# Keys of an attention in chunks of 128, the second head mixing on column halves, the products with the values by even and odd row tiles

## The chip, the cores and the metric

The kernel runs as one program on one core of a Trainium2 chip. The metric is the device time of one execution in microseconds. The times here are a median of several runs; the profile is one further execution of the same program, and its own time stands beside them below.

## What is computed

Attention with talking heads for 4 batches of 12 heads, 448 tokens and 64 columns, and behind it a gated network on all 1792 tokens. All inputs are float32.

```python
scores = scale * np.matmul(q, k.transpose(0, 1, 3, 2))
scores = np.einsum('bhij,hg->bgij', scores, w_pre)
scores = scores - np.max(scores, axis=-1, keepdims=True)
attn = np.exp(scores)
attn = attn / (np.sum(attn, axis=-1, keepdims=True) + 1e-09)
attn = np.einsum('bhij,hg->bgij', attn, w_post)
x = np.matmul(attn, v)            # then (tokens, 12 * 64)
out = (silu(x @ w_gate) * (x @ w_val)) @ w_out
```

## The kernel before

**Stages.** The attention fills about the first 480 us of the span, the gated network the rest. This change is in the attention alone.

**Attention.** For a batch `b`, `qk` (L216) makes the scores of 128 query rows for a pair of heads, `qkcopy` takes them out of PSUM and `store` writes them to a buffer in DRAM. `gather` reads them back so that one row group holds 5 tokens by 12 heads. The work then goes by tiles of 10 query rows (`TS`), two tiles `t` at a time, which is one unit `u`; there are 45 tiles and 23 units a batch, and the last unit has one tile. For each unit: `pre` (L270, first mixing, both tiles at once on quarters of the array), `top` (VectorE, the negated maximum), `expo` (ScalarE, the exponential `e` and its sum), `norm` (VectorE the reciprocal, GpSimd the scaled mixing weights `rw`), `post` (L306, second mixing) and `mixed` (ScalarE, from PSUM into `attnT`).

**Second mixing.** The keys lie in 4 chunks of 112 (`CP`), so that chunk `c` holds the keys p * 4 + c. `post` takes, for each tile and chunk, 112 columns of `e` as the stationary operand and the 120 columns of `rw` as the moving one.

**Values.** `attnT` is a ring of 3 segments of 112 tokens. `av` (L328) multiplies it with the values `vn`, for two segments (224 tokens) and one pair of heads at a time: 4 chunks by 2 heads, the heads on the two column halves of the array, into one buffer of the tag `tr`. The last batch does its last two segments singly. `values` (batches 0, 2, 3) and `second_values` (batch 1) copy the result out of PSUM, on ScalarE and VectorE. The tag `tr` has two buffers in PSUM; `kprep` (L174, name `ktr`) and `qprep` (L191, `qtr`), which transpose the keys and the queries of the next batch, use it too.

**Order.** `at(key, fn)` records every step with a key, and the program is written out in the order of the keys; each engine then runs its own instructions in that order, and waits for semaphores. A unit `u` of a batch has the key n = 45 b + 2 u, which the following calls a slot. In a slot: `pre` at n + 0.5, `qk` of the next rows at n + 0.65, `post` of the unit before at n + 1.2, the transposes at n + 1.25, `av` at n + 1.3, `values` from n + 1.9. The products of the first two segments begin in slot 13 of their batch, with two pairs of heads in that slot and one in each of the next four; those of the last two run in slots 1 to 5 of the next batch.

**Loads.** All loads and stores are issued by SyncE (SP), in order. `load_v` (L144) brings the values of 3 heads, and runs four times from n0 + 16.9 on (n0 = 45 b), one call every 1.95. `load_k` (L162) brings the next batch's keys for a pair of heads, two slots ahead of `kprep`; its tile `kn` has two buffers, so the load for pair p waits until `kprep` has read pair p - 2. In the listings of the order below, `[waits DMAHW3_49]` is a wait for a DMA: there are eight such semaphores, taken in turn, and a DMA on SP that takes one waits until the DMA eight places before it has landed.

## Time and profile before

| | |
|---|---|
| median of 3 runs | 999.2 us (998.84 to 1002.1) |
| the profiled execution | 991.94 us, its span 990.2 us |
| PE (TensorE) busy | 951.3 us, 96% of the span |
| VectorE, ScalarE, GpSimd busy | 642.2, 429.1, 248.1 us |
| granted TensorE clock, mean | 0.996 |
| second mixing on PE (L306) | 1440 records, 170.8 us |
| products with the values on PE (L328) | 864 records, 81.6 us |
| DMA rs<-s_d in the chain that ended last | 3% of the span |

The busy time of PE is no measure of how close PE is to its limit, since records overlap: what a group of matmuls costs is read from where it starts to where the next group starts. Each float32 matmul stands in the trace as two records. PEld is the loading of stationary operands. SPq rows are DMA issues; their length is the time of issuing alone.

### The profile page before, as it was taken

What the parts mean: (1) busy time and instruction counts of PE and PEld (TensorE: products, weight loads), DVE (VectorE), ACT (ScalarE), POOL (GpSimd) and SP (SyncE); (2) the same over time, 40 slices, a digit from 0 to 9 for tenths busy, and PEclk for the clock granted to TensorE, in tenths of its full rate; (3) what the DMA queues carried; (4) which work ended last, traced back from release to release, by engine and by line L of the source; (5) the groups of instructions that cost most, each with busy time, mean ns of one, the idle gap of its engine ahead of it and who ended that gap; (6) DMA issues with size and microseconds to landing.
All of it is one profiled execution on the core that took longest, in us unless ns stands there. A gap on an engine that the chain in (4) does not pass through costs nothing.

```text
span 990.2 us, 18171 instructions
## 1 busy us (share of the span) xinstructions
PE 951.3 (96%) x6732; PEld 757.2 (76%) x6732; DVE 642.2 (65%) x1130; ACT 429.1 (43%) x961; POOL 248.1 (25%) x308
## 2 busy tenths in 40 slices
PE   4699999999999999999999999999999999999998
PEld 2356666656656666667899999999998999999998
DVE  2466555545555564567599999999927999984110
ACT  1366566646565564656334334332223444442110
POOL 2011111133331111122244434443313333320000
PEclk9899999999999999999999999999999999999999
DMA  6799888999799676884255454459663112122311
GB/s 174 212 280 263 260 246 254 269 239 318 223 326 251 204 219 181 244 226 131 80 171 164 144 179 156 144 187 339 235 238 98 61 65 65 65 65 65 118 38 38
DMA packets 146292, 179.03 MB, mean 181 GB/s; under 512 B 51640, under 2 KB 121628, under 8 KB 146204
## 3 DMA queue, kind: packets, MB, share of 16 engines
q1 hardware_dynamic: 145948, 177.77, 59.4%
q8 instruction: 54, 0.88, 0.4%
q14 instruction: 34, 0.28, 0.1%
q0 software_dynamic: 256, 0.09, 0.0%
HBM read 108.59 MB, written 69.24 MB: 180 GB/s over the span
## 4 chain that ended last, share of the span: by engine, by line
PE 84%; DMA 7%; DVE 3%; ACT 2%; SPq 2%; POOL 1%; issue 1%; ACTq 0%; POOLq 0%; DVEq 0%
PE post L306 13%; PE pre L270 7%; PE qk L216 7%; PE dn L731 6%; PE dn L733 6%; PE dn L732 6%; PE av L328 6%; PE p L641 5%; PE p L644 5%; PE p L642 5%; DMA rs<-s_d 3%; PE upv L701 3%; PE upv L696 3%; PE upv L697 3%; PE upg L701 3%; PE upg L696 3%
## 5 line engine op out<-in xcount | busy, mean ns | idle before, releaser
L306 PEld LDWEIGHTS post<-rw,e 128*112 128x112 f32 x1440 | 153.7, 177 | 65.9 <-issue 42.7
L306 PE MATMUL post<-rw,e 128*112 128x120 f32 (+1 forms) x1440 | 170.8, 272 | 6.1 <-POOL rw L298 3.8
L287 ACT ACTIVATE e<-pre,st 128x448 f32<-128x448 f32 x180 | 112.4, 629 | 109.8 <-DVE st L281 109.2
L298 POOL TENSOR_SCALAR rw<-w_post_gs,st 128x120 f32<-128x120 f32 x180 | 67.8, 388 | 338.3 <-DVE st L295 185.3
L281 DVE TENSOR_REDUCE st<-pre 128x1 f32<-128x448 f32 x180 | 104.1, 618 | 63.1 <-PE pre L270 62.4
L731 PE MATMUL dn<-whi,gh 128*128 128x256 f32 x504 | 141.1, 280 | 1.4 <-DVE u L648 1.4
L732 PE MATMUL dn<-wlo,gh 128*128 128x256 f32 x504 | 141.0, 280 | 0.0
L733 PE MATMUL dn<-whi,gl 128*128 128x256 f32 x504 | 141.0, 280 | 0.0
L552 POOL TENSOR_SCALAR mag<-mag 128x768 f32<-128x768 f32 x33 | 99.5, 3015 | 140.9 <-ACT mag L550 137.5
L270 PE MATMUL pre<-rs,w_pre_blocks 60*64 60x448 f32 x720 | 101.3, 565 | 11.1 <-DMA rs<-s_d 8.4
L315 ACT ACTIVATE attnT<-post 112x480 f32<-112x480 f32 (+3 forms) x192 | 97.0, 550 | 13.3 <-PE post L306 9.1
L731 PEld LDWEIGHTS dn<-whi,gh 128*128 128x128 f32 x504 | 94.7, 188 | 1.6 <-DVE u L648 1.6
L732 PEld LDWEIGHTS dn<-wlo,gh 128*128 128x128 f32 x504 | 94.7, 188 | 0.0
L733 PEld LDWEIGHTS dn<-whi,gl 128*128 128x128 f32 x504 | 94.7, 188 | 0.0
L216 PE MATMUL qk<-kk,qt 64*128 64x448 f32 (+1 forms) x384 | 87.9, 583 | 3.9 <-DVE stg L223 1.9
L328 PE MATMUL av<-attnT,vn 112*64 112x224 f32 (+1 forms) x864 | 81.6, 336 | 0.0
L223 DVE COPY stg<-qk 128x448 f32<-128x448 f32 x124 | 72.9, 614 | 6.4 <-PE qk L216 6.4
L216 PEld LDWEIGHTS qk<-kk,qt 64*128 64x128 f32 (+1 forms) x384 | 26.8, 174 | 57.3 <-issue 35.4
L328 PEld LDWEIGHTS av<-attnT,vn 112*64 112x64 f32 x864 | 54.4, 136 | 17.7 <-issue 0.8
L580 DVE TENSOR_TENSOR wlo<-w,whi 128x768 fp32r<-128x768 f32 x48 | 45.5, 950 | 29.7 <-ACT whi L584 29.4
L584 ACT ACTIVATE whi<-w 128x768 fp32r<-128x768 f32 x48 | 40.0, 838 | 36.8 <-PE dn L733 21.2
L687 ACT ACTIVATE gh<-m 128x448 fp32r<-128x448 f32 x36 | 20.9, 579 | 76.3 <-DVE m L712 68.9
(117 smaller groups left out, 1650.8 us busy)
## 6 DMA issues: line engine op xcount, KB each, us to landing
rs<-s_d SPq DMA_DIRECT2D x176, 210.0 KB, 4.7
s_d<-stg SPq DMA_DIRECT2D x72, 448.0 KB, 4.0
w_d<-w SPq DMA_DIRECT2D x36, 384.0 KB, 2.7
w<-w_d SPq DMA_DIRECT2D x36, 384.0 KB, 3.6
raw<-in_moe_w_gate_dram SPq DMA_DIRECT2D x12, 768.0 KB, 4.8
raw<-in_moe_w_val_dram SPq DMA_DIRECT2D x12, 768.0 KB, 4.8
raw<-in_moe_w_out_dram SPq DMA_DIRECT2D x12, 768.0 KB, 5.1
kn<-in_k_dram SPq DMA_DIRECT2D x24, 224.0 KB, 5.2
```

What stands on the lines that cost most here:

```text
L216: nc.tensor.matmul(pt[x][i * m:(i + 1) * m], qt[b, c][hs, p, :m], kk[b, p][hs], start=True, stop=True)
L223: nc.vector.tensor_copy(stg[b, c, g][:, x], pt)
L270: nc.tensor.matmul(pt[r][x * HB:(x + 1) * HB], wpre[i], xs[i, x], start=True, stop=True)
L281: nc.vector.tensor_reduce(sts[b, u][:, 0, r:r + 1], pts[b, t], axis=AX.X, op=ALU.max, negate=True)
L287: nc.scalar.activation(e, pts.pop((b, t)), AF.Exp, bias=st[:, 0, r:r + 1], scale=1.0, accum_out=st[:, 1, r:r + 1])
L306: nc.tensor.matmul(pt[:, c, :, :m], e[:, c * CP:(c + 1) * CP], w[:, :, :m], start=True, stop=True)
L315: nc.scalar.activation(attnT[:, :, :, i:i + m].rearrange("p c h i -> p (c h) i"), pt[:, :, :, done:done + m].rearrange("p c h i -> p (c h) ...
L328: nc.tensor.matmul(pt[j * D:(j + 1) * D], vn[b][:, 2 * p + j, c], ring[:, c, 2 * p + j, segs[0]:segs[-1] + 1:max(1, segs[-1] - segs[0])], ...
L552: eng.tensor_scalar(mag, mag, f32_of(0x38000000), f32_of(0x47EFFFFF), op0=ALU.max, op1=ALU.min)
L731: nc.tensor.matmul(pt, gh, hi, start=opens, stop=False)
L732: nc.tensor.matmul(pt, gh, lo, start=False, stop=False)
L733: nc.tensor.matmul(pt, gl, hi, start=False, stop=closes)
```

## The change

- The keys lie in chunks of 128, 128, 128 and 64. `load_k` becomes two DMAs, one of 3 chunks (key p * 3 + c) and one of the last 64 keys. `load_v` becomes six: four of 3 heads with three chunks, and two that bring the last 64 keys of all 12 heads, once to the lower 64 partitions and once to the upper.
- `post` comes in two parts. Part 0 does the first three chunks of each tile as two matmuls of 64 stationary columns, whose results go to the two partition halves of one buffer. Part 1 does the last chunk of both tiles, one tile on each half, and both results stand in the even tile's buffer.
- `mixed` copies 4 chunks for the even tile (which takes the odd tile's last chunk along, to the upper partitions) and 3 for the odd one, which now comes first.
- Segments have 120 tokens, that is 12 tiles, and the last has 88. `av` makes the even tiles and the odd tiles of a range apart, each in its own buffer of `tr`, so it holds both. The moving operand is up to 12 runs of 10 elements. In the last chunk the even tiles use the lower 64 rows of the array and the odd ones the upper. For the last batch's single segments two pairs of heads go in one call.
- `spread` gives the copies out of PSUM: one for even tiles and one for odd ones (four where the ring wraps), where there was one (two).
- In a slot the transposes now stand ahead of `post` (n + 1.15 against n + 1.2), and one pair of heads is done in each slot, so six slots in a row have an `av`.

```diff
 def load_v(b, c):
...
+        if c < NC:
+            hs = slice(c * (H // NC), (c + 1) * (H // NC))
+            nc.sync.dma_start(
+                out=vn[b][:, hs, :NC - 1].rearrange("p h c d -> p h (c d)"),
+                in_=v[b, hs, :full].rearrange("h (p c) d -> p h (c d)", c=NC - 1),
+            )
+        else:
+            r = c - NC
+            nc.sync.dma_start(
+                out=vn[b][r * HB:(r + 1) * HB, :, NC - 1], in_=v[b, :, full:].rearrange("h p d -> p h d")
+            )
...
 def load_k(b, p):
...
         nc.sync.dma_start(
-            out=t.rearrange("p c j d -> p (c j) d"), in_=k[b, 2 * p:2 * p + 2].rearrange("j (p c) d -> p c j d", c=NC)
+            out=t[:, :NC - 1].rearrange("p c j d -> p (c j) d"),
+            in_=k[b, 2 * p:2 * p + 2, :full].rearrange("j (p c) d -> p c j d", c=NC - 1),
         )
+        nc.sync.dma_start(out=t[:PART, NC - 1], in_=k[b, 2 * p:2 * p + 2, full:].rearrange("j p d -> p j d"))
...
-    def post(b, t):
-        m = rows(t)
-        e = et.pop((b, t))
-        w = rw.pop((b, t))
-        pt = ps.tile([CP, NC, H, TS], F32, tag="post", name=f"post_{b}_{t}")
-        for c in range(NC):
-            nc.tensor.matmul(
-                pt[:, c, :, :m], e[:, c * CP:(c + 1) * CP], w[:, :, :m], start=True, stop=True
-            )
-        ats[b, t] = pt
+    def post(b, u, part):
+        for r, t in enumerate(tiles_of(u)):
+            m = rows(t)
+            e, w = et[b, t], rw[b, t]
+            if part == 0:
+                ats[b, t] = ps.tile([P, NC, H, TS], F32, tag="post", name=f"post_{b}_{t}")
+                for c in range(2 * (NC - 1)):
+                    c, x = divmod(c, 2)
+                    nc.tensor.matmul(
+                        ats[b, t][x * HB:(x + 1) * HB, c, :, :m], e[:, c * P + x * HB:c * P + (x + 1) * HB],
+                        w[:, :, :m], start=True, stop=True,
+                    )
+            else:
+                nc.tensor.matmul(
+                    ats[b, 2 * u][r * HB:(r + 1) * HB, NC - 1, :, :m], e[:, (NC - 1) * P:], w[:, :, :m],
+                    start=True, stop=True,
+                )
+                et.pop((b, t)), rw.pop((b, t))
...
     def av(b, c0, m, p):
...
         for c in range(NC):
-            for j in range(2):
-                nc.tensor.matmul(
-                    pt[j * D:(j + 1) * D], vn[b][:, 2 * p + j, c],
-                    ring[:, c, 2 * p + j, segs[0]:segs[-1] + 1:max(1, segs[-1] - segs[0])],
-                    start=(c == 0), stop=(c == NC - 1),
-                )
+            for x in range(3 - m):
+                for r in range(2):
+                    k = (n + 1 - r) // 2
+                    part, side = (slice(r * HB, (r + 1) * HB), 0) if c == NC - 1 else (slice(P), r)
+                    for j in range(2):
...
+                            a = line[part, c, h, u0:u0 + k, side]
+                        nc.tensor.matmul(o, vn[b][part, h, c], a, start=(c == 0 and x == 0), stop=(c == NC - 1 and x == 2 - m))
...
-        for c in range(NC):
+        for c in range(NC + 2):
             at(n0 + 16.9 + 1.95 * c, later(load_v, b, c))
...
-            at(n + 1.25, later(kprep, b, p))
-            at(n + 1.45, later(kcopy, b, p))
+            at(n + 1.15, later(kprep, b, p))
+            at(n + 1.27, later(kcopy, b, p))
...
-            first = (-(-(c0 + m) * CP // TS) - 1) // 2 + 2
-            for p in range(NPAIR):
-                u = first + (max(0, p - 1) if m == 2 else p // 2)
+            first = (-(-(c0 * SEG + cols(c0, m)) // TS) - 1) // 2 + 2
+            for p in range(0, NPAIR, 3 - m):
+                u = first + p // (3 - m)
```

On PE, slot 13 of batch 0, where that batch's products begin, stood like this from the second mixing to the first `av`s; in a name the first number is the batch, then the tile's or the pair's (`ktr_1_2` is pair 2 of batch 1, `post_0_24` is tile 24 of batch 0).

```order
L306 MATMUL post_0_24_915<-rw_0_24_874,e_0_24_858 112x120 [waits PE_49,Activation_49,Pool_49]
L306 MATMUL post_0_24_915<-rw_0_24_874,e_0_24_858 112x120 x3
L306 MATMUL post_0_25_920<-rw_0_25_876,e_0_25_860 112x120 [waits Activation_49,Pool_49]
L306 MATMUL post_0_25_920<-rw_0_25_876,e_0_25_860 112x120 x3
L174 MATMUL ktr_1_2_931<-ident_104,kn_1_2_792 128x112 [waits DMAHW2_49]
L174 MATMUL ktr_1_2_931<-ident_104,kn_1_2_792 128x112 x3
L328 MATMUL av_0_0_0_936<-attnT_115,vn_0_650 64x224 [waits DVE_49]
L328 MATMUL av_0_0_0_936<-attnT_115,vn_0_650 64x224 x7
L328 MATMUL av_0_0_1_945<-attnT_115,vn_0_650 64x224 [waits DVE_49]
```

Now, from the transposes on, with the last waits of the `av` (rows of it between are left out):

```order
L185 MATMUL ktr_1_2_1001<-ident_107,kn_1_2_862 128x128 [waits DMAHW2_49]
L185 MATMUL ktr_1_2_1001<-ident_107,kn_1_2_862 128x128 x2
L185 MATMUL ktr_1_2_1001<-ident_107,kn_1_2_862 128x64 [waits DMAHW3_49]
L310 MATMUL post_0_24_1006<-rw_0_24_962,e_0_24_937 64x120 [waits Activation_49,Pool_49]
L310 MATMUL post_0_24_1006<-rw_0_24_962,e_0_24_937 64x120 x5
L310 MATMUL post_0_25_1013<-rw_0_25_964,e_0_25_939 64x120 [waits Activation_49,Pool_49]
L310 MATMUL post_0_25_1013<-rw_0_25_964,e_0_25_939 64x120 x5
L315 MATMUL post_0_24_1006<-rw_0_24_962,e_0_24_937 64x120
L315 MATMUL post_0_24_1006<-rw_0_25_964,e_0_25_939 64x120
L367 MATMUL av_0_0_0_0_1030<-attnT_118,vn_0_700 64x120 [waits DVE_49]
L367 MATMUL av_0_0_0_0_1030<-attnT_118,vn_0_700 64x120
...
L367 MATMUL av_0_0_0_0_1030<-attnT_118,vn_0_700 64x120 [waits DMAHW3_49]
L367 MATMUL av_0_0_0_1_1031<-attnT_118,vn_0_700 64x120 [waits DMAHW1_49]
```

The transposes of pair 2 moved ahead of `post`, and the first `av` has at its end two waits for DMAs, which are those of the two `load_v` calls for the last 64 keys, as the next listing shows.

On SP, ahead of that place, the loads and gathers stood like this (`kn` keys, `vn` values, `rs` gathered scores, `qn` queries):

```order
L251 DMA rs_0_14_844<-s_d0_67 60x2x448 [waits DMAHW7_49]
L162 DMA kn_1_3_847<-in_k_dram 112x8x64 [waits DMAHW0_49,PE_49]
L251 DMA rs_0_15_888<-s_d0_67 60x2x448 [waits DMAHW1_49]
L251 DMA rs_0_15_888<-s_d0_67 60x2x448 [waits DMAHW2_49]
L162 DMA kn_1_4_891<-in_k_dram 112x8x64 [waits DMAHW3_49,PE_49]
L152 DMA qn_1_1_893<-in_q_dram 128x12x64 [waits DMAHW4_49]
```

Now:

```order
L170 DMA kn_1_3_924<-in_k_dram 128x6x64 [waits DMAHW1_49,PE_49]
L174 DMA kn_1_3_924<-in_k_dram 64x2x64 [waits DMAHW2_49]
L153 DMA vn_0_700<-in_v_dram 64x12x64 [waits DMAHW3_49]
L253 DMA rs_0_15_972<-s_d0_67 60x2x448 [waits DMAHW4_49]
L253 DMA rs_0_15_972<-s_d0_67 60x2x448 [waits DMAHW5_49]
L170 DMA kn_1_4_975<-in_k_dram 128x6x64 [waits DMAHW6_49,PE_49]
L174 DMA kn_1_4_975<-in_k_dram 64x2x64 [waits DMAHW7_49]
L160 DMA qn_1_1_978<-in_q_dram 128x12x64 [waits DMAHW0_49]
L153 DMA vn_0_700<-in_v_dram 64x12x64 [waits DMAHW1_49]
```

Each load of keys became two DMAs, and the two loads of the last 64 keys' values stand behind those of pair 3 and pair 4, each of which waits for PE.

At the very start SP issued 6 loads of keys and then the first queries without a wait:

```order
L162 DMA kn_0_118<-in_k_dram 112x8x64 x6
L152 DMA qn_0_0_127<-in_q_dram 128x12x64
L152 DMA qn_0_1_129<-in_q_dram 128x12x64
L231 DMA s_d0_67<-stg_0_0_0_168 128x896 [waits DMAHW0_49,DVE_49,Activation_49]
L231 DMA s_d0_67<-stg_0_0_1_183 128x896 [waits DMAHW1_49,DVE_49]
```

Now the first queries are the 13th DMA:

```order
L170 DMA kn_0_121<-in_k_dram 128x6x64 [waits DMAHW0_49]
L174 DMA kn_0_121<-in_k_dram 64x2x64 [waits DMAHW1_49]
L170 DMA kn_0_121<-in_k_dram 128x6x64 [waits DMAHW2_49]
L174 DMA kn_0_121<-in_k_dram 64x2x64 [waits DMAHW3_49]
L160 DMA qn_0_0_136<-in_q_dram 128x12x64 [waits DMAHW4_49]
```

These five stand behind eight without a wait, and each of them waits until the DMA eight before it has landed.

## Rows read from the trace of the kernel before

**Rows 1.** Page, first part: busy us, share of the span, instructions.

```profile
PE 951.3 (96%) x6732; PEld 757.2 (76%) x6732; DVE 642.2 (65%) x1130; ACT 429.1 (43%) x961; POOL 248.1 (25%) x308
```

**Rows 2.** Busy time by stretch: us, engines (instructions), clock, DMA share, GB/s.

```profile
350.00:400.00 50.00, 50.00 (x403) 30.59 (x399) 27.27 (x68) 29.20 (x76) 7.41 (x21) 1.00 0.62 191
```

**Rows 3.** Waits of PE, then of SP: us in total, times, longest.

```profile
PE pre L270 <- DMA rs<-s_d: 8.4, 5, 4.3
...
SPq L162 <- PE ktr L174: 11.3, 7, 2.7
```

**Rows 4.** Timeline of PE in one slot of batch 1: start, us, instructions.

```profile
200.28 1.89 PE L306 MATMUL post<-rw,e 128*112 128x120 f32 x16
202.01 0.55 PE L174 MATMUL ktr<-ident,kn 112*128 112x112 f32 x4
202.49 3.25 PE L328 MATMUL av<-attnT,vn 112*64 112x224 f32 x32
205.66 0.98 PE L270 MATMUL pre<-rs,w_pre_blocks 60*64 60x448 f32 x8
```

**Rows 5.** Timeline of PE where the attention ends.

```profile
473.14 1.03 PE L306 MATMUL post<-rw,e 128*112 128x96 f32 x8 [1.36 <-POOL rw L298]
473.95 0.45 PE L696 MATMUL upv<-x,whi 128*128 128x448 f32 x1
...
476.55 5.07 PE L328 MATMUL av<-attnT,vn 112*64 112x112 f32 x96
481.55 1.48 PE L701 MATMUL upv<-x,whi 128*128 128x448 f32 x6
```

**Rows 6.** Timeline of PE, the last records of an `av` and what follows.

```profile
205.00 0.74 PE L328 MATMUL av<-attnT,vn 112*64 112x224 f32 x6
205.66 0.61 PE L270 MATMUL pre<-rs,w_pre_blocks 60*64 60x448 f32 x4
```

**Rows 7.** The start: first DMA issues of SP, first work of PE.

```profile
0.72 5.32 SPq L162 DMA_DIRECT2D kn<-in_k_dram  x6
...
12.00 0.87 PE L191 MATMUL qtr<-ident,qn 128*128 128x128 f32 x3 [12.00 <-DMA qn<-in_q_dram]
```

**Rows 8.** From issue to landing: all `kn` loads, then two single `qn` loads.

```profile
DMA to landing us min/median/max: 3.1/5.2/8.3
...
DMA to landing us min/median/max: 5.9/5.9/5.9
...
DMA to landing us min/median/max: 6.7/6.7/6.7
```

**Rows 9.** Timeline of SP around slot 13 of batch 0: DMA issues.

```profile
88.35 0.63 SPq L162 DMA_DIRECT2D kn<-in_k_dram  x1
89.02 1.14 SPq L251 DMA_DIRECT2D rs<-s_d  x2
93.04 0.62 SPq L162 DMA_DIRECT2D kn<-in_k_dram  x1
93.71 0.69 SPq L152 DMA_DIRECT2D qn<-in_q_dram  x1
```

**Rows 10.** Timeline of PE over the same time.

```profile
90.73 1.89 PE L306 MATMUL post<-rw,e 128*112 128x120 f32 x16
92.46 0.55 PE L174 MATMUL ktr<-ident,kn 112*128 112x112 f32 x4
```

**Rows 11.** Timeline of PE, the first mixing behind its wait of 4.32 us.

```profile
31.90 2.69 PE L270 MATMUL pre<-rs,w_pre_blocks 60*64 60x448 f32 x8 [4.32 <-DMA rs<-s_d]
```

**Rows 12.** Busy time by stretch: around that wait, and one of batch 1.

```profile
30.00:31.00 1.00, 0.00 (x0) 0.00 (x0) 0.00 (x0) 0.00 (x0) 0.00 (x0) 0.50 0.83 253
36.00:38.00 2.00, 1.29 (x5) 0.59 (x4) 1.49 (x4) 0.63 (x3) 0.00 (x0) 0.83 0.17 67
...
214.00:218.00 4.00, 2.40 (x22) 2.27 (x24) 1.75 (x4) 2.74 (x8) 1.32 (x2) 1.00 0.31 77
```

**Rows 13.** Busy time by stretch, batch 1 from slot 11 to slot 13.

```profile
188.00:206.00 18.00, 16.35 (x132) 10.54 (x134) 7.94 (x20) 9.69 (x27) 3.27 (x9) 1.00 1.09 262
```

More of the change, by code (lines that the diff above doesn't have):

```diff
@@ L122, in talking_heads_moe_kernel @@
     nc.gpsimd.memset(wpost, 0.0)
[L123 removed]
+    attnT = cst.tile([P, NC, H, NSEG * SEG], F32, name="attnT")
     def mixing_consts():
@@ L321, in av, with cols @@
+        if t % 2:
+            copy(slice(P), slice(NC - 1))
+        elif t + 1 < NTB:
+            copy(slice(P), slice(NC))
+        else:
+            copy(slice(P), slice(NC - 1))
+            copy(slice(HB), slice(NC - 1, NC))
+    def cols(c0, m):
+        return min(m * SEG, S - c0 * SEG)
     def av(b, c0, m, p):
-        pt = ps.tile([P, S], F32, tag="tr", name=f"av_{b}_{c0}_{p}")[:, :m * CP].rearrange("p (s i) -> p s i", s=m)
+        n = -(-cols(c0, m) // TS)
+        w = SEG // (3 - m)
+        pt = [ps.tile([P, S], F32, tag="tr", name=f"av_{b}_{c0}_{p}_{r}")[:, :SEG] for r in range(2)]
@@ new lines, in av, with spread @@
+        avs[b, c0, p] = pt, c0, m, wrapped
+    def spread(av, *to):
+        pt, c0, m, wrapped = av
+        n = -(-cols(c0, m) // TS)
+        for r in range(2):
+            k = (n + 1 - r) // 2
+            if wrapped:
+                v = pt[r].rearrange("p (s u i) -> p s u i", s=2, i=TS)
+                for s in range(2):
+                    yield v[:, s], *(
+                        d[:, 0].rearrange("p (s u r i) -> p s u r i", s=2, r=2, i=TS)[:, 1 - s, :, r] for d in to
+                    )
+                continue
+            v = pt[r].rearrange("p (x u i) -> p x u i", x=3 - m, i=TS)
+            width = to[0].shape[-1]
+            g = k if (2 * k - 1 + r) * TS <= width else k - 1
+            last = min(g, width // (2 * TS))
+            yield v[:, :, :last], *(
+                d[:, :, :2 * last * TS].rearrange("p x (u r i) -> p x u r i", r=2, i=TS)[:, :, :, r] for d in to
+            )
+            o = (2 * last + r) * TS
+            rest = min(TS, width - o)
+            if last < k and rest > 0:
+                yield v[:, :, last, :rest], *(d[:, :, o:o + rest] for d in to)
@@ L365, in operand @@
-    def operand(nm, c0, m, c, src, step, order=None):
-        if step == 0:
-            xs = os[nm] = xsp.tile([P, 2, 2, CP], F32R, tag="xs", name=f"xs_{nm}_{c0}_{c}")[:, :, :m]
-            for o, i in order or [(slice(None), slice(None))]:
-                nc.scalar.activation(xs[:, 0, i], src[:, o], AF.Copy)
+        keep_x(x_o["b11" if k == 0 else "b21"][:, c * P:(c + 1) * P, t0:t0 + n], xs[:, :, :n])
+        xf = xtp.tile([P, 1, 2 * SEG], F32, tag="x_b12", name=f"xf_{c0}_{p}", bufs=2)
+        for v, h in spread(av, xf):
+            nc.scalar.activation(h, v, AF.Copy)
@@ new lines, in values, with keep_x, operand @@
+        nc.sync.dma_start(out=x_f[k, c * P:(c + 1) * P, t0:t0 + n], in_=xf[:, 0, :n])
+    def keep_x(dst, xs):
+        nc.sync.dma_start(out=dst.rearrange("x p t -> p x t"), in_=xs.bitcast(F32))
+    def operand(nm, c0, m, c, src, step, av=None):
+        n = cols(c0, m)
+        if step == 0:
+            xs = os[nm] = xsp.tile([P, 2, 2 * SEG], F32R, tag="xs", name=f"xs_{nm}_{c0}_{c}")[:, :, :n]
+            if av:
+                for v, h in spread(av, xs[:, 0:1]):
+                    nc.scalar.activation(h, v, AF.Copy)
+            else:
+                nc.scalar.activation(xs[:, 0], src, AF.Copy)
@@ L494, in talking_heads_moe_kernel @@
                 for step, y in enumerate((1.9, 2.3, 2.5, 2.9)):
-                    at(n + y + (0.7 if p == 1 else 0), later(second_values, c0, m, x, step))
+                    at(n + y, later(second_values, c0, m, x, step))
     LEAD = 0.9
```

138 lines of the change are left out of this document (67 added, 71 removed).

## The prediction, made before the changed kernel was run

> **What bounds the kernel now.** I read the page first: PE is busy for 96% of the span, no other engine for more than 65% [rows 1]. Then the busy time by stretch: where the attention runs undisturbed, PE is busy for the whole 50 us, at the full clock, with the DMA engines at 0.62 [rows 2]. So in most slots a microsecond taken from PE is a microsecond of the result. Then the waits: PE waited 8.4 us for gathers, and SP 11.3 us for PE's transposes, because a load of keys needs the tile that they read [rows 3]. That second one costs nothing now, but it says which queue stands still behind PE. Last the timeline of PE in a slot, for the price of each step [rows 4]. The gated network behind the attention keeps its order, so the result is what the attention gains or loses.
>
> **Second mixing.** From `post` to the transposes 1.73 us pass [rows 4] for 16 records, that is 8 matmuls of 112 by 120, 0.108 a record. Now there are 14 matmuls of 64 columns, in pairs on two halves. That a pair costs one is shown by `av`, which already has its heads on the halves: 96 records of 112 moving columns take 5.00 us [rows 5], so 48 pairs of records at 0.104. I take 0.108 for the 120 columns: 7 pairs are 14 steps, 1.51 us, 0.22 less. Full units: 22 in each of 4 batches, 88 times 0.22 is **-19 us**. The 45th tile of a batch has 4 steps for its matmuls as before.
>
> [...]
>
> **Products with the values.** Two `av`s take 3.17 us [rows 4], 1.585 each, 16 steps of 0.198 for both. Now an `av` has 14 shorter steps: for the 3 full chunks the even and the odd tiles apart, for the last chunk both at once on the row halves, as `pre` runs on quarters. At 120 columns 14 times 0.108 is 1.51, 0.07 less; with 110 and 100 columns (the last two segments of batches 1 and 2) some 1.37, 0.21 less. 30 and 12 of them: -2.1 and -2.5, **-4.6 us**. The last batch's singles were 12 times 0.83 (5.00 us for six [rows 5]); now 6 calls of 28 steps. By columns (60 of 112) a step is 0.056, 1.6 a call and 9.4 together; at no less than 0.104 it would be 17.5. I take 10, no change, since the load has 64 columns against the 112 that fit into `post`'s 0.108; the range keeps +7.5.
>
> What the moving operand costs in runs of ten is not shown. Nearest is the last tile of a batch, 12 runs of 8: 8 records in 0.81 us, 0.101 each [rows 5], where `post`'s 0.108 scaled to 96 columns is 0.086. But that record also loads 112 columns, so the runs cost between 0 and 0.015 a step; 42 calls of 14 steps make 0 to +8.8. I take 0, since the load explains it. [...] No run here shows it alone.
>
> **Change of form.** From the last three pairs of `av` to `pre` 0.66 us pass [rows 6], 0.07 more than three steps; with the load that then lies bare I take 0.15 (0.08 to 0.2). The transposes now stand between `qk` and `post`, not between `post` and what follows, and have a part with 64 rows: one change more in slots with transposes, two in slots 11 and 12, one less in slots with `av` alone. I count +30 in all: **+4.5 us**. PE's sum is -19.
>
> **The start.** PE waits until 12.00 us for the first queries [rows 7]. They were the 7th DMA; now they are the 13th and wait for the 5th (pair 2's keys) to land. Six issues took 5.32 us, 0.89 each; the 5th starts at some 2.6 and lands after the median of 5.2 [rows 8], so the queries go out near 7.7 and not at 6.1: **+1.5 us** (0 to 2.5).
>
> **The new wait in slot 13.** Here I expect the gain to go. The products of a batch begin in slot 13. Before, `load_v` went by heads, and what came last was wanted by the last pairs, slots later. Now its last two DMAs bring the last 64 keys of *all* heads, so the first `av` wants them. The second is behind pair 4's keys on SP, which wait for pair 2's transposes, in this same slot. In the trace this load was issued at 93.04, and the transposes began at 92.46 [rows 9, 10]. From the end of the transposes SP issues the keys (0.62, and some 0.5 for the new second DMA), the queries (0.69) and then the values: 1.9 us with the steps between. Landing took 5.9 and 6.7 us for the queries that will be just ahead of it in the queue, in batches 0 and 1, and 3.1 to 8.3 for loads of keys [rows 8]. PE has `post` (1.51) and three chunks of `av` (12 steps, 1.3) to do, 2.9 with a change of form. The wait is 1.9 + 5.9 to 6.7 - 2.9, or 4.9 to 5.7; by the ends of the keys' row 2.1 to 7.3. I take 5.3 in batches 0, 1 and 2, whose slot 13 has transposes, and 1.6 in batch 3, where no load of keys stands ahead: **+17.5 us**. Behind the wait are all of PE's later steps; nothing hides it.
>
> **The clock.** [...] In batch 1 PE stood for over 1.6 of 4 us at the full clock [rows 12]. [...] I take 1.5 for each of three: **+4.5 us** (0 to 7).
>
> **Gathers in slots 11 to 13.** Here the DMA engines are full (1.09) and PE already waits [rows 13]: of 18 us it is busy for 16.35. SP issues without a pause, two more DMAs for keys come ahead of the gather of unit 13, and PE arrives earlier, so these waits grow by what PE gained there: **+3 us** over four batches (1 to 5). The wait of batch 1 behind slot 13 can shrink, as the DMA queue empties while PE stands: **-1.5**.
>
> **What costs nothing.** More copies out of PSUM (two of 120 columns for one of 224) lie on ScalarE and VectorE, each about 27 to 31 us busy in 50 [rows 2]; if that cover went, the exponentials would be late next. That `av` now holds both `tr` buffers makes it wait for the copy of the transposed keys; `post` lies between, and without it up to 0.4 us would be bare in some 18 slots.
>
> **The sum.** -19 + 1.5 + 17.5 + 4.5 + 3 - 1.5 is +6. The profiled execution took 991.9 us, so it would take 998; the median of the runs stands 7.3 higher at 999.2, and the forecast is **1005 us** there.
>
> **The rivals.** *The load lands in time (faster).* Its place is the same wait; it decides from a landing of some 4 us down. At the 3.1 that one load of keys took, the wait is 2.1, the clock stays (as in the 4 us of batch 1), and the terms are -19 + 1.5 + 6.9 + 0 + 2 - 1 = -10: 990. For it: the queue may be emptier than in the row, as PE comes later; against it: 5.9 and 6.7 in the very place, and 1.09 of the DMA engines. Chance 0.28. *Runs of ten cost 0.015 a step (slower).* The forecast plus 8.8: 1014. For it the row of 8 records, against it the 112 columns of their load. Chance 0.1. *Gain and loss cancel:* the waits of slot 13 are 5 us, but later waits of PE shrink behind them, and the clock stays: -19 + 1.5 + 16.5 + 2 - 1.5 is 0, 999. Chance 0.12. *The halves' loads do not overlap:* a step would be up to twice as long, 88 times 14 times 0.108, or 133 us more, 1132. Rows 5 exclude it nearly; chance 0.01. [...]
>
> **How the numbers follow.** The forecast, 997 to 1013, has 0.49, of which 0.11 lies within 0.3% (3 us, about what a measurement of this kernel can tell from no change). Faster by more is the first rival, 0.28; within is 0.11 and 0.12, 0.23; slower is the rest, 0.49. The range 989 to 1016 takes in the first rival's time and the runs' cost; what lies beyond is a wait that disappears (below) or the ends of several terms together.
>
> **What would show it.** Right: `post` at about 1.5 us for 28 records of 64 columns; 3 waits of PE at `av` for `vn`, 4 to 6 us each, in the slots where batches 0 to 2 begin their products; half the clock behind some of them; first work of PE near 13.5. Wrong: no wait for `vn` (then 983), or an `av` of over 1.65 us without a wait (then the runs cost), or waits that moved to ScalarE.

## The result, and the profile of the changed kernel

The changed kernel takes **1014.4 us** (median of 4 runs, 1013.2 to 1015.5) against 999.5 for the kernel before (4 runs, 998.8 to 1002.1): a ratio of 1.0144, 95% interval 1.0121 to 1.0167. It is slower by 14.9 us where 5.8 were forecast. The direction and its place were right, the size was not. Its profiled execution took 1015.5 us, its span is 1013.7 us; that of before took 991.9.

The page of the changed kernel first: engines, the granted clock in tenths for 40 slices of the span, and the two groups of PE that the change is about (busy us, mean ns of one, idle before them).

```profile
PE 951.1 (94%) x8676; PEld 757.9 (75%) x8676; DVE 642.9 (63%) x1211; ACT 429.0 (42%) x1034; POOL 246.9 (24%) x308
...
PEclk9699899979999799999999999999999999999999
...
L310 PE MATMUL post<-rw,e 128*64 128x120 f32 x2160 | 133.8, 274 | 2.7 <-POOL rw L300 2.3
...
L367 PE MATMUL av<-attnT,vn 128*64 128x120 f32 (+9 forms) x1728 | 89.5, 260 | 23.6 <-DMA vn<-in_v_dram 21.0
```

The busy time of PE is what it was (951.1 against 951.3, [rows 1]), so it says nothing of the change: records overlap (in the rows of slot 13 below, the 24 of `post` end at 212.23 and the next start at 212.07). The news is in the idle time of `av`, which was 0, and in the clock's dips: one at the start, and three in later slices of the attention. PE's waits of the changed kernel (total, times, longest), to be held against [rows 3]:

```profile
PE av L367 <- DMA vn<-in_v_dram: 21.0, 6, 4.6
PE qtr L202 <- DMA qn<-in_q_dram: 13.7, 1, 13.7
PE pre L272 <- DMA rs<-s_d: 7.9, 5, 4.2
```

The forecast wait is there, but six times and not three. Slot 13 of batch 1 on PE, the place of [rows 4] (start, length, and in brackets the idle time before):

```profile
210.78 1.45 PE L310 MATMUL post<-rw,e 128*64 128x120 f32 x24
212.07 0.38 PE L315 MATMUL post<-rw,e 128*64 128x120 f32 x4
212.27 1.40 PE L367 MATMUL av<-attnT,vn 128*64 128x120 f32 x24
216.30 0.42 PE L367 MATMUL av<-attnT,vn 64*64 64x120 f32 x4 [2.63 <-DMA vn<-in_v_dram]
221.29 0.47 PE L367 MATMUL av<-attnT,vn 64*64 64x120 f32 x2 [4.57 <-DMA vn<-in_v_dram]
```

`post` has 28 records and takes 1.49 us to the start of `av` (212.27 less 210.78), where 1.73 stood in [rows 4]. The first three chunks of `av` run, then PE waits for the first load of the last 64 keys, and again for the second. Together that is 7.8 us in batch 0, 7.2 here and 6.0 in batch 2; batch 3 has none. On SP, just before:

```profile
207.81 0.62 SPq L170 DMA_DIRECT2D kn<-in_k_dram  x1
208.48 0.68 SPq L174 DMA_DIRECT2D kn<-in_k_dram  x1
209.20 0.60 SPq L153 DMA_DIRECT2D vn<-in_v_dram  x1
209.85 2.02 SPq L253 DMA_DIRECT2D rs<-s_d  x2
211.96 0.94 SPq L170 DMA_DIRECT2D kn<-in_k_dram  x1
212.94 1.70 SPq L174 DMA_DIRECT2D kn<-in_k_dram  x1
214.68 0.60 SPq L160 DMA_DIRECT2D qn<-in_q_dram  x1
215.39 2.19 SPq L153 DMA_DIRECT2D vn<-in_v_dram  x1
```

and the landing of the two loads of the last 64 keys in 205 to 222 us (issues, KB, median us to landing):

```profile
vn<-in_v_dram SPq DMA_DIRECT2D x2, 192.0 KB, 5.9
```

SP issues here without a pause. The transposes of pair 2 end at 210.86, as `post` begins (210.78); SP comes to pair 4's keys at 211.96, needs 2.7 us for their two loads (1.4 for pair 3's) and issues the second load of the last 64 keys at 215.39, 4.5 us behind the transposes. In batches 0 and 2 it is 5.1 and 2.9 us; in batch 2 SP reached pair 4's keys just as the transposes ended (330.94 and 330.91). In [rows 9] SP had stood idle from 90.16 until the transposes let it go at 93.04. A second hold lies at the end of it: count back eight DMAs from 215.39 (the `rs` row holds two), and that is pair 3's large load, whose landing at 215.38 frees the semaphore that the two share. It adds 0.1 us here, and 0.5 and 0.7 us in batches 2 and 0. The values landed 5.9 us after their issue, and PE went on at 221.29.

The clock, by the granted clock of four stretches (busy times of the engines, PEclk, DMA share, GB/s):

```profile
32.50:49.50 17.00, 12.88 (x55) 5.69 (x55) 5.21 (x12) 3.71 (x10) 1.43 (x4) 0.50 0.75 224
...
100.80:110.90 10.10, 5.14 (x23) 1.98 (x23) 2.21 (x5) 2.33 (x8) 0.00 (x0) 0.50 0.85 197
216.90:227.00 10.10, 5.71 (x28) 2.57 (x30) 3.41 (x9) 2.16 (x7) 0.78 (x2) 0.50 0.60 162
336.30:346.40 10.10, 6.22 (x32) 3.08 (x34) 3.49 (x10) 1.68 (x6) 0.61 (x2) 0.50 0.53 140
```

Behind each of the three double waits PE works 5 to 6 us at a granted clock of 0.50. In batch 0 a `qk` there takes 1.80 us to the start of what follows it (108.51 to 110.31), and 0.95 in the next slot, at 1.00 (115.23 to 116.18). By that, an estimate, the work would have taken about half as long, so this execution lost some 2.6, 2.9 and 3.1 us. At the start the stretch is 17 us long with 12.9 us busy, against 6.8 us with 4.5 busy before ([rows 12] lie inside it), which by the same estimate cost this execution some 4 us more. Most of that is not the change's: second profiles of the two kernels (e10 and e13 below) have 9.0 and 8.1 us busy there.

By the starts of `pre` in both traces, the changed kernel is 4.0 us behind in the first slot and 6.8 in the third, gains 2.1 until slot 13 of batch 0, loses 7.7 to 8.5 in two slots at the start of the products of batches 0, 1 and 2, and gains 2.8 to 3.8 from the end of each batch to that place in the next. What PE gains, it gains in all slots; what it loses lies in a few.

### The profile page after: what moved, and what is told of

Read it like the earlier page. It is cut to its first block, busy times and chain, and to the rows that moved or that the text cites. A ratio compares the mean times of both kernels' runs of the same rounds, so it can differ in the third digit from the quotient of the medians.

```text
span 1013.7 us, 22277 instructions
## 1 busy us (share of the span) xinstructions
PE 951.1 (94%) x8676; PEld 757.9 (75%) x8676; DVE 642.9 (63%) x1211; ACT 429.0 (42%) x1034; POOL 246.9 (24%) x308
## 4 chain that ended last, share of the span: by engine, by line
PE 63%; DMA 5%; DVE 3%; ACT 2%; POOL 1%; issue 1%; SPq 1%; ACTq 0%; POOLq 0%; DVEq 0%
PE dn L798 6%; PE dn L799 6%; PE dn L800 6%; PE p L708 5%; PE p L711 4%; PE p L709 4%; PE post L310 4%; PE pre L272 4%; PE av L367 3%; PE upv L763 3%; PE upv L768 3%; PE upv L764 3%; PE upg L763 3%; PE qk L227 3%; PE upg L768 3%; PE upg L764 3%
## 5 line engine op out<-in xcount | busy, mean ns | idle before, releaser
L310 PEld LDWEIGHTS post<-rw,e 128*64 128x64 f32 x2160 | 112.6, 139 | 40.0 <-issue 22.3
L310 PE MATMUL post<-rw,e 128*64 128x120 f32 x2160 | 133.8, 274 | 2.7 <-POOL rw L300 2.3
L272 PE MATMUL pre<-rs,w_pre_blocks 60*64 60x448 f32 x720 | 105.8, 577 | 12.7 <-DMA rs<-s_d 7.9
L367 PE MATMUL av<-attnT,vn 128*64 128x120 f32 (+9 forms) x1728 | 89.5, 260 | 23.6 <-DMA vn<-in_v_dram 21.0
L367 PEld LDWEIGHTS av<-attnT,vn 128*64 128x64 f32 (+1 forms) x1728 | 73.1, 136 | 35.1 <-DMA vn<-in_v_dram 22.8
L328 ACT ACTIVATE attnT<-post 128x360 f32<-128x360 f32 (+3 forms) x184 | 85.6, 522 | 29.2 <-PE post L310 25.4
L227 PE MATMUL qk<-kk,qt 64*128 64x448 f32 (+1 forms) x384 | 94.8, 609 | 3.1 <-DVE qt L209 1.4
L234 DVE COPY stg<-qk 128x448 f32<-128x448 f32 x124 | 72.9, 615 | 12.4 <-PE qk L227 12.3
L227 PEld LDWEIGHTS qk<-kk,qt 64*128 64x128 f32 (+1 forms) x384 | 29.2, 183 | 57.6 <-issue 37.6
```

Source lines behind the costliest of these rows:

```text
L227: nc.tensor.matmul(pt[x][i * m:(i + 1) * m], qt[b, c][hs, p, :m], kk[b, p][hs], start=True, stop=True)
L234: nc.vector.tensor_copy(stg[b, c, g][:, x], pt)
L272: nc.tensor.matmul(pt[r][x * HB:(x + 1) * HB], wpre[i], xs[i, x], start=True, stop=True)
L310: nc.tensor.matmul(ats[b, t][x * HB:(x + 1) * HB, c, :, :m], e[:, c * P + x * HB:c * P + (x + 1) * HB], w[:, :, :m], start=True, stop=True,)
L328: nc.scalar.activation(attnT[ps, cs, :, i:i + m].rearrange("p c h i -> p (c h) i"), pt[ps, cs, :, :m].rearrange("p c h i -> p (c h) i"), A ...
L367: nc.tensor.matmul(o, vn[b][part, h, c], a, start=(c == 0 and x == 0), stop=(c == NC - 1 and x == 2 - m))
```

## The experiments

Each ratio is to the kernel before, run on the same chip beside the experiment; its medians there were 998.2 to 998.5 us.

**The late loads go first.** One line of the plan, the same six loads:

```diff
-        for c in range(NC + 2):
-            at(n0 + 16.9 + 1.95 * c, later(load_v, b, c))
+        for i, c in enumerate((0, NC, NC + 1, 1, 2, 3)):
+            at(n0 + 16.9 + 1.95 * i, later(load_v, b, c))
```

> The changed kernel (1014.4), with the two loads of the last 64 keys' values issued second and third of the six, ahead of the other heads, and nothing else. Theory (the wait for values makes the loss): PE's three double waits for vn (7.8, 7.2 and 6.0 us, 21.0 in the profile) go, and so do the stretches at half the clock behind them, some 2.5 us each; the gathers of slots 11 to 13, behind two more loads, take back 2 to 4. Some 25 us less: 990 (986 to 995). Rival (the DMA engines are full there, and PE only waits elsewhere): the vn waits come back as waits of pre for rs, 1005 or more. Rival (the loss is in PE's steps, runs of ten or forms): PE's records fill the time, 1010 or more.

Measured: 992.1 us, ratio 0.9951 (0.9926 to 0.9975). 22 us less than the changed kernel by the medians, 19 by the ratios, and faster than the kernel before. No wait for `vn` is left. Slot 13 now runs through; batch 0, from `post` to the next `pre`:

```profile
93.62 1.45 PE L310 MATMUL post<-rw,e 128*64 128x120 f32 x24
94.90 0.38 PE L315 MATMUL post<-rw,e 128*64 128x120 f32 x4
95.11 1.77 PE L367 MATMUL av<-attnT,vn 128*64 128x120 f32 x32
96.69 0.97 PE L272 MATMUL pre<-rs,w_pre_blocks 60*64 60x448 f32 x8
```

An `av` takes 1.58 us to the start of `pre`, change of form included. So most of the loss is neither in PE's steps nor in gathers; it is these two loads and what stands behind them.

**The queries back to 7th place.**

```diff
-            at(min(ready[0] - 8, -54 + c) if b == 0 and c < 2 else ready[0] - 8, later(load_q, b, c))
+            at(-57.5 + 4.5 * c if b == 0 and c < 2 else ready[0] - 8, later(load_q, b, c))
```

> The changed kernel with batch 0's first queries issued after three pairs of keys, so as 7th DMA, as before the change, and the second queries as 12th. Theory (the start is worth far more than my 1.5 us, because the queries are late and PE warms up later): the first qtr returns from 13.7 to some 12, unit 2's pre comes 4 to 7 us earlier, 1014.4 becomes 1009 (1007 to 1011). Rival (my term): 1.5 us, 1013. Rival (the keys behind the queries are late instead): 1014 or more.

Measured: 1010.8 us, ratio 1.0145 (1.0111 to 1.0179). By the medians 3.6 us less, by the ratios nothing, so this run alone doesn't settle it. Its profile has the first `qtr` at 9.48 us and the first `pre` at 30.64, where the changed kernel had 13.73 and 35.91.

**Both.** The two edits together.

> Both edits of the two runs before together. Theory (independent terms): the gains add, 990 less 5 is 985 (981 to 990), which is 14 below the kernel before, about the PE savings of my sum (second mixing 19, products 4.6, less the change of form 4.5) less what the gathers take. Rival (a later limit, the gathers or the clock, takes part of it back): 990 or more. Rival (the gain of PE is not there): 999 or more.

Measured: 987.1 us, ratio 0.9907 (0.9875 to 0.9939). Beside e1 the edit at the start is worth 5.0 us by the medians and 4.4 by the ratios, three times my term. The first `pre` shows the same gain; e1, then e3_both:

```profile
35.74 2.63 PE L272 MATMUL pre<-rs,w_pre_blocks 60*64 60x448 f32 x8 [4.21 <-DMA rs<-s_d]
```

```profile
31.09 2.65 PE L272 MATMUL pre<-rs,w_pre_blocks 60*64 60x448 f32 x8 [4.17 <-DMA rs<-s_d]
```

The stretch at half clock behind it is as long in both (10.2 us; in e3_both the granted clock from 30 to 45 us is 0.66), so the gain is not in that stretch. The time is slower than the 985 expected, though inside its range. Two waits that were small in the changed kernel (0.6 us for `kk`, 2.3 for `e`) have grown, and the profile names them:

```profile
PE pre L272 <- DMA rs<-s_d: 7.9, 7, 4.2
PE av L367 <- DVE kk L193: 5.1, 1, 5.1
PE pre L272 <- ACT e L289: 4.9, 2, 3.8
```

The 5.1 us are in batch 1: `av` needs the `tr` buffer of the transposed keys, which VectorE has not copied. VectorE waits for `e` at this time (5.20 us), and ScalarE, ahead of `e`, for a store; in batch 3 ScalarE waits for raw weights:

```profile
208.78 0.40 ACT L431 ACTIVATE xs_t<-xb 128x240 fp32r<-128x240 f32 x1 [4.77 <-DMA x_t<-xs_t]
...
418.56 0.89 ACT L617 ACTIVATE mag<-raw 128x768 f32<-128x768 f32 x1 [5.74 <-DMA raw<-in_moe_w_gate_dram]
```

**PE kept busy while it waits.** 26 matmuls whose results nobody reads, ahead of the first `av` of batches 0 to 2:

```diff
+        if c0 == 0 and p == 0 and b < 3:
+            for i in range(26):
+                nc.tensor.matmul(pt[i % 2], ident, ident[:, :SEG], start=True, stop=True)
```

> The changed kernel with 26 extra matmuls (128 by 128 by 120, of the identity, results unused) ahead of the first product with values in slot 13 of batches 0, 1 and 2, some 0.2 us each, 5.2 us, which fit in the waits for vn (7.8, 7.2, 6.0). They do no work; the values still land when they land. Theory (the waits cost the clock, and this costs 2 to 3 us each): the waits shrink to 1 to 3 us, the granted clock stays at 1.00 behind them, and the time falls by 6 to 9 us: 1006. Rival (my term of 1.5 each): by 4.5, 1010. Rival (the clock falls all the same, or costs nothing): 1014.

Measured: 1012.6 us, ratio 1.0159 (1.0125 to 1.0192). The waits for `vn` fell to 2.3 us in all and two of the three stretches at half clock were gone (mean granted clock 0.989, where the changed kernel's profile had 0.974), yet the median fell by 1.8 us only. So it was run again, beside the changed kernel.

> The changed kernel itself, beside the next run on the same chip: 1014.4 (1.0144 of before), mean granted clock 0.974 to 0.980.

> The kernel of e4_filled once more, with more rounds. There the waits and the half clock behind them went in the profile (the attention ended 7.6 us earlier), but the median fell by 1.8 us only. Theory (the clock is worth 6 to 9 us and those four executions were slow behind the attention): 6 us or more below e10_after_again. Rival (my term, 1.5 each): 4.5. Rival (what the clock gives is taken back in the network, or the network's clock differs from execution to execution by as much): 2 or less.

Measured: the changed kernel 1013.0 us, ratio 1.0152 (1.0128 to 1.0177), and the filled one 1008.6 us, 1.0101 (1.0078 to 1.0125). 4.4 us apart, with intervals that don't touch: my own term of the prediction, not the theory of 6 to 9. The stretch behind batch 1's wait, filled:

```profile
216.90:227.00 10.10, 9.56 (x120) 6.22 (x122) 6.08 (x17) 5.63 (x18) 3.66 (x7) 1.00 0.64 206
```

The clock is whole there. That the gain is less than the 8.5 us read from the first profile's rows has two reasons. In the second profile of the changed kernel the stretches behind the waits are 10.2, 6.8 and 6.8 us and no longer 10.2 each, with 14.2 us busy, worth 7.1. And the filled kernel ran longer at half clock at the end of the attention:

```profile
441.50:448.40 6.90, 5.77 (x44) 4.04 (x46) 5.10 (x13) 4.46 (x15) 0.71 (x2) 0.51 0.60 154
485.90:489.30 3.40, 3.20 (x19) 2.81 (x20) 0.00 (x0) 1.60 (x3) 0.15 (x1) 0.50 0.12 26
```

The changed kernel has 3.5 us busy at half clock there, so the filled one loses 5.5 / 2 = 2.7 us again, and 7.1 less 2.7 is the 4.4 measured. That is one profile of each, and why the end is slower isn't shown. How long the clock stays down differs between executions of the same program (behind batch 1's waits 10.2 and 6.8 us); one profile doesn't give its price.

**One load moved up.** The second of the two late loads directly behind the first, so ahead of two gathers, pair 4's keys and the queries, by its key alone:

```diff
-            at(n0 + 16.9 + 1.95 * c, later(load_v, b, c))
+            at(n0 + 16.9 + 1.95 * c - 0.75 * (c == NC + 1), later(load_v, b, c))
```

> The changed kernel (1014.4), with the second of the two loads of the last 64 keys' values at the key n0 + 25.9, so right behind the first and ahead of pair 4's keys; the first stays where it is, behind pair 3's keys. Theory (the late issue of the second load, behind the transposes of the same slot and behind the landing of the DMA eight places before, makes most of the wait): the first wait stays (3.4, 2.6, 1.5 us), the second shrinks to under 1 us, so the waits fall from 21.0 to some 9 and the stretches at half the clock get shorter: 1001 (997 to 1004). Rival (both land late because the DMA engines are full there): the waits stay above 17, 1012.

Measured: 996.2 us, ratio 0.9972 (0.9943 to 1.0000), 18 us less than the changed kernel and a little more gain than the 997 to 1004 expected. The waits for `vn`:

```profile
PE av L367 <- DMA vn<-in_v_dram: 5.1, 4, 2.9
```

Slot 13 of batch 0 shows both waits, 2.92 and 0.17 us:

```profile
100.54 0.42 PE L367 MATMUL av<-attnT,vn 64*64 64x120 f32 x4 [2.92 <-DMA vn<-in_v_dram]
101.13 0.32 PE L367 MATMUL av<-attnT,vn 64*64 64x120 f32 x2 [0.17 <-DMA vn<-in_v_dram]
```

Behind these 2.9 us the granted clock stayed at 1.00 (97 to 106 us). So the first load costs little where it is; the place of the second, behind pair 4's keys and the queries, is most of the loss (18 us by the medians, where e1 gave 22 for both).

**The wait alone, in the kernel before.** Its four loads by chunks for all heads, the last at the place of the changed kernel's last:

```diff
-        hs = slice(c * (H // NC), (c + 1) * (H // NC))
...
+        nc.sync.dma_start(out=vn[b][:, :, c], in_=v[b].rearrange("h (p c) d -> p h c d", c=NC)[:, :, c])
...
-            at(n0 + 16.9 + 1.95 * c, later(load_v, b, c))
+            at(n0 + 16.9 + 1.95 * c + 3.9 * (c == NC - 1), later(load_v, b, c))
```

> The kernel before (998.4), where load_v goes by chunk of 112 keys for all 12 heads in place of 3 heads with all chunks, and the fourth such load is issued at the key n0 + 26.65, behind pair 4's keys, as the last value load of the changed kernel is. PE's steps are those of before. Theory (a load for all heads in that place is by itself the loss): waits of PE at av for vn of 4 to 7 us in slot 13 of batches 0 to 2, half the clock behind each for 2 to 3 us, 998.4 becomes 1019 (1013 to 1025). Rival (it takes the changed kernel's many DMAs as well, two for each pair of keys, which fill the eight DMA semaphores): waits under 3 us, 1005 or less.

Measured: 1027.3 us, ratio 1.0296 (1.0252 to 1.0341), 29 us more, out of the expected range on the far side. With one load and one DMA for a pair of keys, the waits are 4.9 to 5.3 us, close to the 5.3 that I had forecast for one load:

```profile
PE av L324 <- DMA vn<-in_v_dram: 15.0, 3, 5.3
```

Here SP waits for the transposes and issues the load at 99.42, 1.4 us after the keys' (98.03), with only the queries' load in between. That is the path of the prediction, which had 1.9 us of issues there; the changed kernel's waits are longer because its SP has more to issue and is late when the transposes end. (The values come in pieces of 64 elements here, and of 256 in the kernel before.) That 15 us of waits cost 29 was more than expected: around each the clock is down twice (0.51 and 0.50 in 3.5 and 6.8 us of batch 0), 26.8 us of PE's work in all six stretches and so some 13 us, and PE waits longer for gathers too (12.3 us against 8.4).

**Runs of ten.** The operand of the first three chunks in one run:

```diff
+                            if c < NC - 1:
+                                o = pt[r][js, x * SEG // 2:x * SEG // 2 + k * TS]
+                                a = attnT[:, c, h, first * SEG:first * SEG + k * TS]
```

(and likewise where the ring wraps)

> The kernel of e3_both, with the moving operand of the first three chunks of av read as one run of up to 120 elements and no longer as 12 runs of 10 (it then takes tokens of both parities, so the products are others; the last chunk keeps its runs). 12 of 14 steps of 36 calls are priced by it. Theory (runs of ten cost nothing, the term that I took): 987, slots with av stay at 5.57 and 4.71 us. Rival (0.015 a step, the other end of my bound): 36 x 12 x 0.015 is 6.5 us less, 980.5, and slots with av are 0.18 us shorter.

Measured: 986.9 us, ratio 0.9888 (0.9844 to 0.9931), against 987.1 and 0.9907. An `av` takes 1.59 us to the next `pre`, as it does in e3_both:

```profile
108.72 1.77 PE L373 MATMUL av<-attnT,vn 128*64 128x120 f32 x32
110.31 0.93 PE L272 MATMUL pre<-rs,w_pre_blocks 60*64 60x448 f32 x8
```

Runs of ten floats cost nothing here, so the rival that priced them is out.

**The transposes back behind the second mixing**, on e3_both:

```diff
-            at(n + 1.15, later(kprep, b, p))
-            at(n + 1.27, later(kcopy, b, p))
+            at(n + 1.25, later(kprep, b, p))
+            at(n + 1.45, later(kcopy, b, p))
```

(the queries' likewise, and the second part of `post` directly behind the first)

> The kernel of e3_both with the transposes back behind the second mixing, as before the change (and the second part of post directly behind its first). Theory (what I said in the prediction: av holds both tr buffers and then has nothing between it and the copy of the transposed keys; up to 0.4 us bare in some 18 slots, which is 7, less some 0.07 to 0.15 for each of 30 changes of form saved): 2 to 5 us more, 990. Rival (the changes of form are the larger): 984.

Measured: 998.2 us, ratio 0.9999 (0.9983 to 1.0016), 11 us more, where 2 to 5 were expected. A slot with `av` and transposes grows from 5.57 to 6.30 us. Most of that is in `av`, which takes 2.22 us to the next `pre` and not 1.59, with a wait in it:

```profile
109.55 0.75 PE L185 MATMUL ktr<-ident,kn 128*128 128x128 f32 x4
110.23 0.43 PE L367 MATMUL av<-attnT,vn 128*64 128x120 f32 x4
111.02 1.61 PE L367 MATMUL av<-attnT,vn 128*64 128x120 f32 x28 [0.36 <-DVE kk L193]
```

The `av` of the odd tiles stands for the copy of the keys. The move of the transposes, whose changes of form I had priced at +4.5 us, is what makes the two buffers of `tr` affordable.

**What is late next.** First a guess that fell, on e3_both: batch 0's products loaded back a slot earlier.

```diff
-                    at(n - 3.0, later(x_back, c0, m, x))
+                    at(n - 5.0, later(x_back, c0, m, x))
```

> The kernel of the run e3_both (987.1, 0.9907 of the kernel before), with x_back in batch 1 (the load of batch 0's products, xb from x_f) two units of the key earlier, so one slot. In e3_both PE still waits 5.1 us once, in batch 1, at av for VectorE's copy of keys kk (its tr buffer), with half the clock behind it. Theory (VectorE stands at second_values for xb, and the copy of keys is queued behind it): the wait goes, 5 to 8 us less, 981 (0.983 to 0.986 of before). Rival (VectorE is late for its own work, or the earlier load takes the time from gathers): 987 (0.990).

Measured: 988.9 us, ratio 0.9916 (0.9886 to 0.9945): nothing gained. PE still waits 4.0 us for `kk`; VectorE was not waiting for that load but for `e`, and ScalarE for the store of `x_t`, as the rows of e3_both above show. I had read VectorE's queue and not followed the chain to its end. So, on e3_both again, the two transfers for which ScalarE waits:

```diff
-    xsp = pool(right, "xsp", 4, "right")
+    xsp = pool(right, "xsp", 5, "right")
...
-                    at(n + x + 0.25, later(convert, u, step))
+                    at(n + x + (2.0 if unit_index(u) == 0 else 0.25), later(convert, u, step))
```

> The kernel of e3_both (987.1, 0.9907 of before) with five buffers of the tag xs in place of four, and the first unit of weights converted 1.75 units of the key later. In e3_both ScalarE stands 4.77 us in batch 1 for the DMA that stores x_t (a buffer of xs comes free with it), and 5.74 us in batch 3 for the first raw weights; PE's 5.1 us wait for kk and its 3.8 us wait for e stand behind these. Theory (those two transfers are what is late next, once the values are in time): both waits go or halve, 4 to 9 us less, 981 (0.982 to 0.987 of before). Rival (the wait moves on to the next late transfer, as it did in e5_products_back_earlier): 987 (0.990).

Measured: **973.1 us, ratio 0.9754 (0.9730 to 0.9779)**, 14 us less than e3_both and the fastest of all: 25 us below the kernel before and 41 below the changed one. The 5.1 us for `kk` are down to 0.6, and `e` costs little:

```profile
PE pre L272 <- DMA rs<-s_d: 5.9, 6, 4.4
...
PE pre L272 <- ACT e L289: 1.4, 3, 0.6
...
PE av L367 <- DVE kk L193: 0.6, 1, 0.6
```

Behind the start its granted clock was 1.00 to the end of the attention (from 400 to 430 us, where PE had waited for `e`, it reads 1.00; the mean of the span is 0.995). Which of the two transfers gives how much isn't shown.

**Does the kernel before gain by that edit too?** The later conversion alone, in the kernel before; a fifth `xs` buffer was not run in it.

> The kernel before with the first unit of weights converted 1.75 units of the key later, as in e9_two_waits. There ScalarE waited 1.68 us for these weights, against 5.74 us in e3_both. Theory (PE of the changed kernel comes to this place earlier, and only then is the transfer late): 0 to 2 us less, 997 (0.998 to 1.000). Rival (most of e9_two_waits' 14 us is this edit, which the kernel before would have got as well): 990 (0.992).

Measured: 996.4 us, ratio 0.9971 (0.9939 to 1.0002): 0 to some 5 us at the interval's end, most likely 2 to 3. So at most some 20 of e9's 25 are the change's own, once nothing stands in its way. Not shown is what the fifth buffer would give the kernel before: there too ScalarE waits for these stores, 12.2 us in 7 times, but PE waits only 1.8 us for `e` and 2.9 for `attnT`, so it is probably little.

**The kernel before, profiled again.**

> The kernel before itself, profiled once more. Theory (the 7.3 us between its first profile, 991.9, and its median are stretches at half the clock that this profile did not have): an execution near 999 has a mean clock of some 0.990 and 10 to 14 us more at half the clock than the 6.83 us of the first profile. Rival (the difference lies in waits for DMAs or in the network): as many stretches as in the first profile, the time lost elsewhere.

Measured: 998.3 us median; the profiled execution took 995.5. It has 10 us at half the clock at the start where the first profile had 6.8, and two stretches more, which in the first profile were at full clock:

```profile
30.60:40.70 10.10, 8.09 (x24) 2.38 (x24) 3.27 (x7) 1.88 (x5) 0.71 (x2) 0.51 0.77 231
218.40:221.70 3.30, 3.30 (x20) 2.75 (x20) 2.73 (x7) 2.95 (x8) 1.30 (x3) 0.51 0.84 286
283.30:286.50 3.20, 3.20 (x13) 1.65 (x11) 2.30 (x5) 2.54 (x8) 1.15 (x3) 0.50 0.96 304
```

It is 3.6 us later than the first profile, and reaches the network 4.1 us later. So about half of the 7.3 us between the first profile and the median are such stretches and the waits ahead of them; what the other half is stays open.

## Why the prediction was right in kind and wrong in size

**Second mixing (-19) and products (-4.6).** Right. `post` takes 1.49 us to `av` (forecast 1.51), `av` 1.58 to 1.59 with its change of form (forecast 1.51 and some 0.07). From the end of a batch to slot 13 of the next, 14 slots, the changed kernel gains 2.8 to 3.8 us; with the 11 slots at the start that is 12.4 us in 53 slots, 0.23 a slot, or 21 in all 91 or so. My -24 with +4.5 for changes of form is -19. The six calls for the last batch's singles took 1.8 to 2.1 us each and not 1.6. The halves do overlap: without that the 14 steps of `post` would have taken up to 3.0 us, an estimate from twice 0.108 a step, and they take 1.49, where the 16 of the kernel before took 1.73 [rows 4].

**The start (+1.5).** This step failed: it ends at PE's first work. The queries came 1.7 us later (13.73 against 12.00), near my 1.5, but by luck: they went out behind twelve issues at 9.12 and not near 7.7 (the 5th load went at 3.60 and not 2.6), with no hold by a semaphore, and landed in 4.5 us where they had taken 5.8. The kernel's time hangs on the first `pre`, and that came 4.0 us later:

```profile
35.91 2.66 PE L272 MATMUL pre<-rs,w_pre_blocks 60*64 60x448 f32 x8 [4.25 <-DMA rs<-s_d]
```

against 31.90 in [rows 11]. The other 2.3 us lie between the first `qtr` and the third `qk` (8.8 us against 6.5): PE does more work at its first, slow speed (the first eight `ktr` take 2.27 us, not 1.70) and stays slow for longer, until 22.2 us and not 16.2; why longer isn't shown. Beside e1, e3_both gains 4.4 to 5.0 us, of which 0.8 is a `pre` earlier than in the kernel before (31.09).

**The wait in slot 13 (+17.5).** The mechanism, the place and the batches were right, the size 3 us short: 21.0 and 20.1 us in two profiles. It is 5 short in the three batches; batch 3 has no such wait, where I had put 1.6. The failed step is "from the end of the transposes SP issues": it takes SP as standing ready there, as it did before. The load goes out 5.1, 4.5 and 2.9 us after the transposes and not 1.9. Of that, 2.4 and 1.1 us in batches 0 and 1 are SP coming late to pair 4's keys: a DMA more for each pair of keys and two more for the values keep it issuing without a pause. In batch 2 it stood ready. The three issues ahead of the load took 2.0, 3.3 and 2.4 us and not 1.9, and 0.7, 0.1 and 0.5 are the semaphore of the DMA eight places before. I had used the eight semaphores for the start and not here, and had counted the added DMAs for the gathers and not for SP's own time. e7 confirms the rest: where SP stands ready the wait is 4.9 to 5.3. The landing was right, 6.1 and 5.9 in batches 0 and 1; in batch 2 PE went on 6.4 us after the issue.

**The clock (+4.5).** No run shows the 1.5 us that the sum has for one wait. In the kernel before, the stretch at a granted clock of 0.50 around the wait of 4.32 us in [rows 11] held 4.5 us of PE's work, worth some 2.2; for the three new waits together the pair e10 and e11 showed 4.4. So the term was right on the median, but by luck in part: the stretches behind the three waits were worth 8.5 and 7.1 by the rows of two profiles, against my three times 1.5, and the filled kernel lost some of it again at the end of the attention.

**Gathers (+3 and -1.5).** No such growth shows: PE waits 7.9 and 8.0 us for gathers in the two profiles of the changed kernel, 8.4 and 7.1 in those of the kernel before.

**What I had at nothing.** Off in batch 3: ScalarE converts the first raw weights ahead of `e` in its queue, and stood 2.5 us for them in the changed kernel; PE waited 2.0 behind that and then ran 3.4 us at half clock. Before, the same wait of 1.7 was hidden from PE. And between the last tile's `post` and the network's first `p` (L708) it fell another 2.0 us behind (20.5 to 22.5), which includes the singles. "If that cover went, the exponentials would be late next" was the right place to look, without a number.

**The offset.** I added 7.3 us, profile to median, to a sum that already counts clock stretches. By e13 a good part of those 7.3 are clock stretches of the kernel before. They are real in its median, so the constant was fair for the base; but the changed kernel has its own, larger, share, and a sum on one undisturbed profile can't tell them apart.

Together: some 2.5 us from the start, 3 from the wait in slot 13, 6 from batch 3 and the end of the attention; against them stand some 2 more gained in the slots and 1.5 for gathers. That is 8 of the missing 9, an estimate from single profiles, and the rest stays open. That e1 gained 22 us by the medians, just the 17.5 and 4.5 of the two terms, hides a trade: the waits were larger, and new ones (5.3 us for `kk`, 4.0 for `e`) took their place.

**The rivals.** "The load lands in time" was out: it took 5.9 and 6.1 us to land, and a load in time is worth what that rival said only when it is issued elsewhere (e1, 992, against its 990). Runs of ten cost nothing (e6). Gain and loss did not cancel.

## What to carry to other kernels

When a load is cut by another axis, ask which consumer is first to need the *last* piece: pieces that each served one later step became two that the first step wants, and moving one DMA up by five places in the queue was worth some 18 us. On a queue that issues in order, a load's time is not that of the wait ahead of it alone: ask whether the queue still stands ready when the wait ends, once every added DMA has its 0.6 us or more. And a faster engine moves the bound to whatever used to arrive just in time; here two transfers for ScalarE, worth 14 us, which showed only once the first wait was gone.

## What the runs showed of the hardware that was not expected

The granted clock can stay down for 10 us behind a wait of 7, with PE busy for 5 to 6 of these, and for another length at the same place in the next execution (10.2 against 6.8 us). Behind 2.9 us of waiting in e8 it stayed whole. At the very start the granted clock reads 1.00 while PE is slow all the same: in the changed kernel this stretch and this row belong together, a `qk` of 1.87 us that takes 1.07 five microseconds later.

```profile
16.00:20.00 4.00, 4.00 (x13) 1.68 (x11) 1.81 (x3) 0.67 (x2) 0.00 (x0) 1.00 0.00 0
```

```profile
17.43 1.87 PE L227 MATMUL qk<-kk,qt 64*128 64x448 f32 x4
...
22.56 1.07 PE L227 MATMUL qk<-kk,qt 64*128 64x448 f32 x4
```

The trace's first record of the clock stands at 22.2 us here, and until then `qk` is slow (16.2 in the kernel before, where the slow ones end too): the view prints 1.00 where it has no record. So a 1.00 in a window near the start is no evidence that PE runs at full speed there; the length of a known record is.
